# The second of two MLPs computed as seven half-size products, with combined weights kept in DRAM

## The chip, the cores and the metric

One core of a Trainium2 chip (trn2) runs the whole program. The metric is the device time of one execution in microseconds (us), from the core's first instruction to its last. The engines named below are TensorE (PE: matrix products; the loads of its weights are a row of their own, PEld), VectorE (DVE), ScalarE (ACT), GpSimd (POOL), and SyncE (SP), whose queue issues nearly all DMAs.

## The reference, cut to what matters

Block-causal attention (4 batches, 8 heads, 576 positions, head size 64; 64-wide blocks) gives x with 2304 tokens of width 512. Then two MLPs of inner width 2048 follow one another:

```python
attn = softmax(where(block_i >= block_j, q @ k.T / 8, -1e9)) @ v      # [4, 8, 576, 64]
x = attn.transpose(0, 2, 1, 3).reshape(2304, 512)
h = x @ moe_w_in;  r = maximum(h, 0)                 # [2304, 2048]
x = (s * (r * r) + b) @ moe_w_out                    # [2304, 512]
h = x @ moe2_w_in; g = maximum(0.01 * h, h)
out = g @ moe2_w_out
```

Inputs of the weights are 64-bit words that hold floating-point numbers; the kernel decodes them to 32 bits on the chip. Every product of the MLPs is carried in a high part and a low part: A B is computed as Ah Bh + Ah Bl + Al Bh, three matmuls for one.

## The kernel before, in words

Tokens are cut into five blocks by position in the sequence: four of 512 columns (4 batches of 128 positions) and one of 256 (NB = 5). The inner width is cut into 16 chunks of 128 (NF = 16). For one block and one chunk, `m_in` (L772) makes the hidden chunk h with 12 matmuls (four slices of 128 inputs, three matmuls each, L782), ACT and DVE apply the activation and split the result into high and low (`gh`, `gl`), and `m_out` (L817) adds it to four output banks y with 12 more (L831). So a chunk is 24 matmuls as wide as the block, and an MLP is 16 chunks of this for each of five blocks.

ORDER (L177) lists the ten blocks: five of the first MLP, in the order 0, 1, 2, 4, 3, then five of the second. While a block of the first MLP runs, the attention of the next block is worked off beside it, 16 pieces for each block (`later_block`, L584); so attention ends before the last block of the first MLP begins. The output of the first MLP is stored to DRAM (yT, L854) and read again by `x_split` (L738).

The weights lie in the pool "w", 16 buffers of 8 KB per partition, one for each chunk. `first_weights` (L323) and `second_weights` (L341) load 512 KB at a time and `chunk` (L268) decodes them: on DVE L275, L278, L286 and L294, on ACT L283 and L291, each over 1024 columns. The second MLP's chunks are loaded and decoded as the first MLP's last block gives up its buffers.

Nothing of this runs in the order in which it is written. `Graph.order` (L71) plays the steps through with an assumed length for each, gives each free engine the ready step with the earliest due time, and writes the steps out in that order; a step that opens a buffer waits until the pool has one free. The order on each engine is then fixed, and each engine works its own list from the top. The pool "st" has two buffers, through which y is evicted and stored.

## Time and profile before

| | |
|---|---|
| runs of the kernel | 993.75, 995.41 and 996.36 us, median 995.41 |
| span of the profiled execution | 995.1 us |
| busy share of the span | PE 99%, PEld 82%, DVE 48%, ACT 45%, POOL 10% |
| mean granted TensorE clock | 0.996 of full |
| DMA traffic | 83.91 MB, mean 84 GB/s |

The page gives the profiled execution by its span alone; the three runs lie around it. In the page's 40 slices of the span PE is at 9 tenths or more in all but the first and the last, and DVE falls from 4 to 9 tenths in the first 25 slices to 1 to 3 in the last 15, where only the second MLP runs.

### The profile page before, as it was taken

The page shows a single profiled execution, that of the slowest core. Times are in us where ns is not written, and L with a number is a line of the kernel's source. Part 1 is how long each engine was busy: PE and PEld are TensorE (multiplying, and loading weights), DVE is VectorE, ACT ScalarE, POOL GpSimd, SP SyncE. Part 2 cuts the span into 40 slices and gives each one's busy share as a digit, 9 for nine tenths or more (in the row PEclk, how much of TensorE's full clock was granted, in tenths as well). Part 3 has the DMA queues.
Part 4 walks back from the last instruction along what each step waited for, and adds up shares of the span by engine and source line. Part 5 has one row for each costly group of instructions (what it writes and reads, how often), then busy time and mean ns, then how long its engine had stood idle before and what let it go on. Part 6 is the DMA issues. An engine that isn't in the chain of part 4 may idle for free.

```text
span 995.1 us, 15325 instructions
## 1 busy us (share of the span) xinstructions
PE 980.2 (99%) x5684; PEld 815.2 (82%) x5684; DVE 478.9 (48%) x973; ACT 448.6 (45%) x975; POOL 99.0 (10%) x233
## 2 busy tenths in 40 slices
PE   9899999999999999999999999999999999999997
PEld 8688887777778888888878888888888888888897
DVE  5899865454566455756547996213112111311221
ACT  4777654454544455666636675213213121321221
POOL 1111411111121111222200000000000000000000
PEclk9999999999999999999999999999999999999999
DMA  8982232222233223433134563002001100200010
GB/s 198 329 282 78 62 112 83 64 57 66 73 107 99 72 83 88 121 105 105 57 107 171 209 222 117 1 1 84 1 1 54 32 1 1 64 1 1 12 32 22
DMA packets 84554, 83.91 MB, mean 84 GB/s; under 512 B 20352, under 2 KB 67584, under 8 KB 84480
## 3 DMA queue, kind: packets, MB, share of 16 engines
q1 hardware_dynamic: 82032, 82.15, 26.9%
q10 hardware_dynamic: 2448, 0.79, 0.3%
q8 instruction: 45, 0.74, 0.3%
q14 instruction: 29, 0.24, 0.1%
HBM read 73.47 MB, written 9.44 MB: 83 GB/s over the span
## 4 chain that ended last, share of the span: by engine, by line
PE 93%; DMA 4%; ACT 1%; SPq 1%; DVE 1%; issue 0%; POOLq 0%; ACTq 0%; DVEq 0%; POOL 0%
PE h L782 40%; PE y L831 39%; PE o L716 5%; PE t L454 4%; PE s L637 2%; DMA early<-in_moe_w_out_dram 2%; PE s L677 1%; PE s L439 1%; DMA fv<-in_v_dram 1%; DMA q<-in_q_dram 1%; DMA fk<-in_k_dram 1%; DVE g L798 0%; ACT g L800 0%; DMA out_dram<-yo 0%; SPq L309 0%
## 5 line engine op out<-in xcount | busy, mean ns | idle before, releaser
L782 PE MATMUL h<-xh,w 128*128 128x512 f32 (+1 forms) x1280 | 444.6, 379 | 3.5 <-ACT w L291 1.2
L831 PE MATMUL y<-gh,w 128*128 128x512 f32 (+2 forms) x1280 | 369.8, 372 | 0.0
L782 PEld LDWEIGHTS h<-xh,w 128*128 128x128 f32 x1280 | 237.7, 189 | 51.9 <-issue 5.3
L831 PEld LDWEIGHTS y<-gh,w 128*128 128x128 f32 x1280 | 230.0, 189 | 40.4 <-issue 1.0
L782 PE MATMUL h<-xl,w 128*128 128x512 f32 (+1 forms) x640 | 236.7, 370 | 0.5 <-DVE xl L552 0.5
L831 PE MATMUL y<-gl,w 128*128 128x512 f32 (+2 forms) x640 | 236.2, 369 | 0.2 <-DVE gl L811 0.2
L811 DVE TENSOR_TENSOR gl<-g,gh 128x512 fp32r<-128x512 f32 (+1 forms) x80 | 51.1, 639 | 275.8 <-ACT g L810 270.1
L809 ACT ACTIVATE gh<-h 128x512 fp32r<-128x512 f32 (+1 forms) x80 | 44.3, 554 | 273.1 <-PE h L782 273.1
L831 PEld LDWEIGHTS y<-gl,w 128*128 128x128 f32 x640 | 120.7, 189 | 20.9 <-DVE gl L811 0.4
L782 PEld LDWEIGHTS h<-xl,w 128*128 128x128 f32 x640 | 121.2, 189 | 17.9 <-DVE xl L552 0.9
L800 ACT ACTIVATE g<-h 128x512 f32<-128x512 f32 (+1 forms) x80 | 44.4, 555 | 109.2 <-PE h L782 102.4
L454 PE MATMUL t<-id_sb,p 128*128 128x128 f32 x400 | 65.2, 278 | 2.7 <-POOL p L656 2.0
L454 PEld LDWEIGHTS t<-id_sb,p 128*128 128x128 f32 x400 | 47.8, 141 | 18.4 <-ACT pt L370 3.3
L803 DVE TENSOR_TENSOR gl<-g,gh 128x512 fp32r<-128x512 f32 (+1 forms) x80 | 50.7, 634 | 12.8 <-ACT gh L802 12.4
L656 POOL TENSOR_SCALAR p<-p,l 128x384 f32<-128x384 f32 (+1 forms) x63 | 40.7, 659 | 159.2 <-DVE l L654 118.7
L798 DVE TENSOR_TENSOR g<-g,h 128x512 f32<-128x512 f32 (+1 forms) x50 | 30.3, 606 | 53.8 <-ACT g L800 53.6
L802 ACT ACTIVATE gh<-g 128x512 fp32r<-128x512 f32 (+1 forms) x80 | 47.0, 587 | 14.9 <-DVE g L798 14.2
L372 DVE COPY pt<-t 128x512 f32<-128x512 f32 (+2 forms) x54 | 31.8, 589 | 40.8 <-PE t L454 40.1
L716 PEld LDWEIGHTS o<-pt,v 128*64 128x64 f32 x896 | 41.4, 138 | 10.3 <-DVE pt L372 2.5
L716 PE MATMUL o<-pt,v 128*64 128x128 f32 (+1 forms) x896 | 48.3, 259 | 0.3 <-ACT pt L370 0.3
L810 ACT ACTIVATE g<-h 128x512 f32<-128x512 f32 (+1 forms) x80 | 44.0, 550 | 0.0
L370 ACT ACTIVATE pt<-t 128x512 f32<-128x512 f32 (+2 forms) x66 | 35.0, 532 | 19.9 <-PE t L454 18.2
(88 smaller groups left out, 884.2 us busy)
## 6 DMA issues: line engine op xcount, KB each, us to landing
early<-in_moe_w_in_dram SPq DMA_DIRECT2D x30, 512.0 KB, 3.8
early<-in_moe_w_out_dram SPq DMA_DIRECT2D x30, 512.0 KB, 4.6
v<-in_v_dram SPq DMA_DIRECT2D x32, 256.0 KB, 3.2
k<-in_k_dram SPq DMA_DIRECT2D x32, 144.0 KB, 2.9
yT<-yo SPq DMA_DIRECT2D x16, 256.0 KB, 2.4
k<-in_k_dram SPq DMA_DIRECT2D x32, 128.0 KB, 2.8
xf<-yT SPq DMA_DIRECT2D x16, 256.0 KB, 2.8
out_dram<-yo SPq DMA_DIRECT2D x16, 256.0 KB, 2.6
```

The source lines that it names most:

```text
L370: e.activation(out=out, in_=in_, func=ACTF.Copy, scale=by)
L454: e.transpose(tb()[:, x * 128:(x + 1) * 128], P()[:, pc:pc + 128], id_sb)
L656: G.add({"POOL": pool(nk), "DVE": dve(nk, 2)}, lambda e, h=h, l=l, P=P: e.tensor_scalar(out=P()[:, nk * h:nk * h + nk], in0=P()[:, nk * h: ...
L716: e.matmul(out=o()[64 * h:64 * h + 64, n * x:n * x + n], lhsT=V()[:, j, 64 * h:64 * h + 64], rhs=r, start=(j == 0), stop=(j == nj - 1),)
L782: e.matmul(out=h()[:, :T], lhsT=w()[:, wi, c * 128:(c + 1) * 128], rhs=x[blk, c]()[:, :T], start=(c == 0 and n == 0), stop=(c == KD - 1 an ...
L800: a = G.add({"ACT": act(T)}, lambda e: e.activation(out=g()[:, :T], in_=h()[:, :T], func=ACTF.Relu), [prev], [g], [h], due)
L802: hi = G.add({"ACT": act(T)}, lambda e: e.activation(out=gh()[:, :T], in_=g()[:, :T], func=ACTF.Copy), [a], [gh], [g], due)
L803: lo = G.add({"DVE": dve(T)}, lambda e: e.tensor_tensor(out=gl()[:, :T], in0=g()[:, :T], in1=gh()[:, :T].bitcast(F32), op=ALU.subtract), [ ...
L809: hi = G.add({"ACT": act(T)}, lambda e: e.activation(out=gh()[:, :T], in_=h()[:, :T], func=ACTF.Lrelu), [prev], [gh], [h], due)
L810: a = G.add({"ACT": act(T)}, lambda e: e.activation(out=g()[:, :T], in_=h()[:, :T], func=ACTF.Lrelu), [prev], [g], [h], due)
L811: lo = G.add({"DVE": dve(T)}, lambda e: e.tensor_tensor(out=gl()[:, :T], in0=g()[:, :T], in1=gh()[:, :T].bitcast(F32), op=ALU.subtract), [ ...
L831: e.matmul(out=y()[:, :W], lhsT=w()[:, wi, d * 128:(d + 1) * 128], rhs=x()[:, :W], start=(f == 0 and n == 0), stop=(f == NF - 1 and n == 2),)
```

## The change

The first MLP, the attention and their blocks stay as they are. The second MLP is computed another way, and the weights are handled another way.

**Seven products instead of eight.** The 2304 columns are taken as three groups j of 768, the inner width as two halves of 1024. A group and a half is one of six steps (STEPS). In a step, both matrix products are cut into 2 x 2 blocks, and Strassen's form (with Winograd's sums) makes the four result blocks from seven block products of 384 columns (NH = 384). One unit of PE work, called a product below, is six matmuls of 384 columns (L1088 for the input side, L1154 for the output side). The input side of a step is four groups `in_pair` of seven products; the output side, `out_phase`, is 28 products, seven for each of four groups. So a step is 56 products or 336 matmuls, and the second MLP is 2016 matmuls of 384 columns.

**Sums beside it.** The seven right-hand sides are made on the chip. `x_load` reads four quarters of the group's x for each of two slices and makes seven splits with four differences each: 22 instructions on ACT and 22 on DVE for each j, in 29 buffers "X" that serve one j at a time. For the output side each group needs four differences on DVE and seven splits (ACT the high part gh, DVE the low part gl, L1147 and L1001). Products that share a bank are chained: a bank is copied out by ACT before the next product is added onto it, and other banks are added to the result on DVE (L1063, L1068).

**Weights.** `units` loads the second MLP's weights in 16 units during the first MLP, decodes each, makes seven combinations (on DVE L424, L427, L433, four sums of 256 columns L441, one L448 over 1792 columns; on ACT two instructions), and stores them to DRAM (u_in, u_out, 29.4 MB). `load_units` reads them back in the second MLP, 15 loads of about 1 MB whenever the half changes, four times in all.

**Room.** The pool "w" has 12 buffers in place of 16. Eight of the first MLP's chunks are kept in DRAM too, and each later block reads four of them back (`weights_at`), walking the chunks back and forth. The SBUF of the attention's pools and of the first MLP's is given to the second MLP's pools; `gate` holds the opening of these until every step that uses the old ones has been issued. On the left side the old pools are stg, gh, gl, g, st, xh, xl and the new ones w2, gh2, gl2, Y, G; counted in KB per partition, st lies at 42 to 46 and the first of the 16 buffers of G at 43.5 to 45.

The diff, cut to its core:

```diff
+    def gate(self, fn, keys, new):
+
+        s = self.add({"X": 0.001}, fn, due=-1e9)
+        for u in self.steps:
+            if u is not s and any(b.key in keys for b in u.uses):
+                u.later.append(s)
+                s.left += 1
+        for k in new:
+            self.gates[k] = s
...
-                    dma = max(dma, end + 0.5) + s.nbytes / 220e3
+                    dma = max(dma, end + 0.5) + s.nbytes / 300e3
...
-ORDER = (0, 1, 2, 4, 3, 0, 1, 2, 3, 4)
+ORDER = (0, 1, 2, 4, 3)
...
-    EARLY = NF - 1
+    KEEP = 4
...
+    MLP1 = (("stg", 2), ("gh", 2), ("gl", 2), ("g", 1), ("st", 2), ("xh", 4), ("xl", 4))
+    ATT = (("xf", 4), ("k", 2), ("kh", 1), ("kl", 1), ("q", 3), ("qs", 1), ("v", 3), ("p", 2), ("pt", 3), ("sm", 6))
+    MLP2 = (("w2", 3), ("gh2", 3), ("gl2", 2), ("Y", 4), ("G", 16))
+    XIN = (("X", 29),)
+    open_pools("mlp1", "left", MLP1)
+    open_pools("att", "right", ATT)
...
-    def second_weights():
...
+            if f < KEEP or f >= NF - KEEP:
+                slot = f if f < KEEP else f - NF + 2 * KEEP
+                kept_ok[f] = G.add(
+                    {"SP": 0.65}, lambda e, w=w, slot=slot: e.dma_start(out=kept[slot], in_=w().bitcast(F32).rearrange("p a n -> p (a n)")),
+                    [a], [], [w], due + 8, nbytes=1048576)
...
+    def weights_at(blk, pos, f):
+
+        if not blk:
+            return
+        if pos < NF - KEEP:
+            w_t[blk, f] = w_t[blk - 1, f]
+            for i in range(2):
+                w_ok[blk, f, i] = w_ok[blk - 1, f, i]
+            return
+        slot = f if f < KEEP else f - NF + 2 * KEEP
+        w = w_t[blk, f] = buf("w", [128, 4, 512], F32R, "w")
+        a = G.add(
+            {"SP": 0.65}, lambda e: e.dma_start(out=w().bitcast(F32).rearrange("p a n -> p (a n)"), in_=kept[slot]),
+            [kept_ok[f], done[blk, pos - NF + KEEP]], [w], [], at(blk, pos) - 30, nbytes=1048576)
+        for i in range(2):
+            w_ok[blk, f, i] = a
...
+    def units():
+
+        seq = [(half, kind, i) for half in range(2) for kind in range(2) for i in range(4)]
...
+            slot = buf("stg", [128, 2, 2, 1024], F32, "unit")
...
+            s1 = comb("S1", "A21", "A22", ALU.add, [a])
+            s3 = comb("S3", "A11", "A21", ALU.subtract, [a])
+            s2 = comb("S2", "S1", "A11", ALU.subtract, [s1])
+            s4 = comb("S4", "A12", "S2", ALU.subtract, [s2])
+            hi = G.add({"ACT": act(1792)}, lambda e, c7=c7, h7=h7: e.activation(out=h7().bitcast(F32R), in_=c7(), func=ACTF.Copy), [s3, s4], uses=[slot], due=due)
+            lo = G.add({"DVE": dve(1792)}, lambda e, c7=c7, h7=h7: e.tensor_tensor(out=c7(), in0=c7(), in1=h7(), op=ALU.subtract), [hi], uses=[slot], due=due, port=True)
...
-    second_weights()
...
+    G.gate(lambda e: (close_pools("att"), open_pools("xin", "right", XIN)), [k for k, _ in ATT], [k for k, _ in XIN])
+    G.gate(lambda e: (close_pools("mlp1"), open_pools("mlp2", "left", MLP2)), [k for k, _ in MLP1], [k for k, _ in MLP2])
...
+    ONE = 6 * (NH / 2400 + 0.013)
+    IN_ORDER = (1, 5, 6, 3, 7, 2, 4)
+    STEPS = ((0, 0), (0, 1), (1, 1), (1, 0), (2, 0), (2, 1))
+    t2 = [begin[NB] + n * 56 * ONE for n in range(len(STEPS) + 1)]
...
+    def load_units(n):
+
+        j, half = STEPS[n]
+        if n and STEPS[n - 1][1] == half:
+            for m in (in_w, in_ok):
...
+                w = in_w[n, i, c] = buf("w", [128, 2, 7, 128], F32R, "wi")
+                in_ok[n, i, c] = G.add(
+                    {"SP": 0.65}, lambda e, w=w, u=8 * half + 2 * i + c: e.dma_start(
+                        out=w().bitcast(F32).rearrange("p s r n -> p s (r n)"), in_=u_in[u]),
+                    [*unit_ok[half, 0, i], *gate()], [w], [], t2[n] + 7 * ONE * i - 14, nbytes=917504, behind=line[-1:])
...
+                    raw[a, b] = buf("X", [128, NH], F32, "xr")
+                    row, col = (2 * (a - 1) + c) * 128, 2 * NH * j + NH * (b - 1)
+                    from_ = [y_st[k, 2 * (a - 1) + c] for k in range(NB) if T0[k] < col + NH and T0[k] + TB[k] > col]
+                    t += 0.01
+                    ld = G.add(
+                        {"SP": 0.65}, lambda e, x=raw[a, b], row=row, col=col: e.dma_start(out=x(), in_=yT[row:row + 128, col:col + NH]),
+                        [*from_, in_last[0]], [raw[a, b]], [], t - 4, nbytes=512 * NH)
...
+            a = split(1, x11, [ok[1, 1]])
+            t1 = comb(x11, x12, x11, [a, ok[1, 2]])
+            a = split(5, x11, [t1])
+            tt2 = comb(x11, x22, x11, [a, ok[2, 2]])
+            split(6, x11, [tt2])
+            a = split(2, x21, [ok[2, 1]])
+            t4 = comb(x21, x21, x11, [a, tt2])
+            t3 = comb(x12, x22, x12, [t1, ok[2, 2]])
+            split(7, x12, [t3])
+            split(4, x21, [t4])
+            split(3, x22, [ok[2, 2]])
...
+    def in_pair(n, i):
+
+        j = STEPS[n][0]
+        t = t2[n] + (7 * i + 2 * max(i - 1, 0)) * ONE
+        A, B, C = bank("h" if i % 2 == 0 else "t", "A"), bank("s", "B"), bank("s", "C")
+        where = {1: (A, True), 6: (A, False), 7: (A, False), 4: (A, False), 5: (C, True), 3: (C, False), 2: (B, True)}
...
+            def fn(e, r=r, x=x, first=first, ai=ai):
+                for c in range(2):
+                    hi, lo, _ = x2[j, r, c]
+                    for m, (s, y) in enumerate(((0, hi), (0, lo), (1, hi))):
+                        e.matmul(out=x()[:, :NH], lhsT=in_w[n, i, c]()[:, s, ai], rhs=y(), start=(first and c == 0 and m == 0), stop=(c == 1 and m == 2),
+                                 skip_group_check=True)
+
+            after = [*[in_ok[n, i, c] for c in range(2)], *[x2[j, r, c][2] for c in range(2)]]
+            after += {6: [ev.get(1)], 7: [ev.get(6)], 4: [ev.get(7)], 3: [ev.get(5)]}.get(r, [])
+            p = G.add({"PE": ONE}, fn, after, [x] * first, [x, *[in_w[n, i, c] for c in range(2)], *[q for c in range(2) for q in x2[j, r, c][:2]]], due)
...
+            if r in (1, 5, 6):
+                y = g[{1: (1, 1), 5: (2, 2), 6: (1, 2)}[r]]
+                ev[r] = G.add({"ACT": act(NH)}, lambda e, x=x, y=y: copy(e, y(), x()[:, :NH]), [p], [y], [x], d2)
+            elif r in (2, 3, 7):
+                y = g[{2: (1, 1), 3: (1, 2), 7: (2, 2)}[r]]
+                ev[r] = a = G.add({"DVE": dve(NH)}, lambda e, x=x, y=y: add(e, y(), x()[:, :NH]), [p, ev[{2: 1, 3: 6, 7: 5}[r]]], [], [x, y], d2)
+                ok[{2: (1, 1), 3: (1, 2), 7: (2, 2)}[r]] = G.add(
...
+    def out_phase(n):
...
+                gh, gl = buf("gh2", [128, NH], F32R), buf("gl2", [128, NH], F32R)
+                hi = G.add({"ACT": act(NH)}, lambda e, gh=gh, x=x: e.activation(out=gh(), in_=x(), func=ACTF.Copy), [a], [gh], [x], due - 2)
+                lo = G.add({"DVE": dve(NH)}, lambda e, gh=gh, gl=gl, x=x: sub(e, gl(), x(), gh().bitcast(F32)), [hi], [gl], [gh, x], due - 1.5, port=True)
...
+                def fn(e, r=r, i=i, z=z, first=first, gh=gh, gl=gl):
+                    for d in range(2):
+                        for m, (s, y) in enumerate(((0, gh), (1, gh), (0, gl))):
+                            e.matmul(out=z[d]()[:, :NH], lhsT=out_w[n, r]()[:, 2 * i + d, s], rhs=y(), start=(first and i == 0 and m == 0), stop=(i == 3 and m == 2),
+                                     skip_group_check=True)
...
+                if again and r in last:
+                    store(j, last[r], d, a, due + 2 * ONE)
```

What this does to the order on the engines shows at two places.

The first place is the border between the two MLPs, on ACT. Before, the last rows of the first MLP (y evicted into yo, L370) and the first of the second (L809, L810) follow one another with work for the weights between them:

```order
L802 ACTIVATE gh<-g 128x512 [waits Activation_49]
L283 ACTIVATE early<-early 128x1024 [waits DMAHW7_49,DMAHW6_49,DVE_49]
L370 ACTIVATE yo<-y,s_sb 128x512 [waits PE_49]
L291 ACTIVATE w<-early 128x2x512 [waits DVE_49]
L809 ACT_TABLE_LOAD
L809 ACTIVATE gh<-h 128x512 [waits PE_49]
L810 ACTIVATE g<-h 128x512 [waits Activation_49]
```

Now (the last split of the first MLP, one y, then the first copies of a bank A or C into G):

```order
L892 ACTIVATE gh<-g 128x512 [waits DVE_49]
L479 ACTIVATE yo<-y,s_sb 128x512 [waits DMAHW3_49,PE_49]
L1063 ACTIVATE G<-A 128x384 [waits DMAHW3_49,DMAHW2_49,DMAHW7_49,DMAHW0_49,DVE_49]
L1063 ACTIVATE G<-C 128x384
L1103 ACT_TABLE_LOAD
L1103 ACTIVATE G<-G 128x384 [waits DVE_49]
L1063 ACTIVATE G<-A 128x384 [waits PE_49]
L1147 ACTIVATE gh_7222<-G 128x384 [waits Activation_49]
```

The first copy into G now waits for four DMAs. SP's list at the same place shows which have these four numbers last (wo are weights of the output side, 1 MB each; before, no load stood between the stores of the border that anything on ACT waited for):

```order
L996 DMA wo<-u_out 128x2048 [waits DMAHW6_49,PE_49]
L936 DMA yT<-yo 128x512 [waits DMAHW7_49,DVE_49]
L936 DMA yT<-yo 128x512 [waits DMAHW0_49,Activation_49]
L996 DMA wo<-u_out 128x2048 [waits DMAHW1_49,PE_49]
L936 DMA yT<-yo 128x512 [waits DMAHW2_49,DVE_49]
L936 DMA yT<-yo 128x512 [waits DMAHW3_49,DVE_49]
```

A DMA's own number is the one that it waits for: the copy stands behind all four stores of the last block. On PE three products of the first group stand ahead of the last twelve matmuls of y, one product of the second group behind them, and then the product that needs this copy.

The second place is the change from one group j to the next, on DVE. Before, a change of block in the second MLP put four splits of x and four evictions among one gl for each chunk:

```order
L811 TENSOR_TENSOR gl<-g,gh 128x512 x14
L764 SCALAR_TENSOR_TENSOR xl<-xf,c_sb,xh 128x512 x4
L811 TENSOR_TENSOR gl<-g,gh 128x512
L372 COPY yo<-y 128x512 x2
```

Now, twelve rows of the stretch in which the second j's x is made (xr, xl) beside the output side of the first (gl, Y):

```order
L1001 TENSOR_TENSOR xl_8140<-xr,xh_8128 128x384
L1001 TENSOR_TENSOR gl_8143<-G,gh_8130 128x384
L1001 TENSOR_TENSOR xr<-xr 128x384
L1001 TENSOR_TENSOR G<-G 128x384
L1001 TENSOR_TENSOR xr<-xr 128x384
L1001 TENSOR_TENSOR xl_8160<-xr,xh_8156 128x384
L1001 TENSOR_TENSOR gl_8164<-G,gh_8158 128x384
L1001 TENSOR_TENSOR xr<-xr 128x384
L1001 TENSOR_TENSOR gl_8175<-G,gh_8162 128x384
L1001 TENSOR_TENSOR gl_8179<-G,gh_8166 128x384
L1001 TENSOR_TENSOR xl_8189<-xr,xh_8177 128x384
L1068 TENSOR_TENSOR Y<-A,Y 128x384
```

Four of these twelve are a gl that a product waits for; the rest stand in between. Counted in the lists, DVE has 68 instructions of 384 columns between one gl and the gl of the product 26 products later at each of the two changes of j; where j does not change, some 40 in such a stretch.

## Rows read from the trace of the kernel before

**Rows 1.** The page's chain of work that ended last, by engine.
```profile
PE 93%; DMA 4%; ACT 1%; SPq 1%; DVE 1%; issue 0%; POOLq 0%; ACTq 0%; DVEq 0%; POOL 0%
```
**Rows 2.** Windows: stretch, length, busy us (instructions) of each engine, clock, DMA.
```profile
50.00:100.00 50.00, 49.94 (x263) 40.68 (x258) 45.73 (x68) 38.27 (x65) 7.26 (x17) 1.00 0.53 178
100.00:500.00 400.00, 396.27 (x2785) 324.04 (x2783) 235.83 (x614) 219.69 (x546) 82.46 (x190) 1.00 0.30 84
595.00:989.00 394.00, 393.76 (x1916) 333.23 (x1915) 91.39 (x135) 103.27 (x192) 0.00 (x0) 1.00 0.09 27
```
**Rows 3.** Timeline of PE (start, us, instruction): 18 matmuls of 512, then 24 of 256.
```profile
587.80 0.39 PE L782 MATMUL h<-xh,w 128*128 128x512 f32 x1
...
591.88 0.39 PE L782 MATMUL h<-xh,w 128*128 128x512 f32 x1
...
965.72 0.28 PE L782 MATMUL h<-xh,w 128*128 128x256 f32 x1
...
968.60 0.28 PE L782 MATMUL h<-xh,w 128*128 128x256 f32 x1
```
**Rows 4.** Groups by line and shape: count, busy us, mean ns, idle before.
```profile
L570 DVE TENSOR_TENSOR kl<-k,kh 128x384 fp32r<-128x384 f32 x16 | 8.8, 551 | 0.2 <-ACT kh L569 0.2
L569 ACT ACTIVATE kh<-k 128x384 fp32r<-128x384 f32 x16 | 8.2, 511 | 0.0
```
**Rows 5.** Timeline of DVE: instructions that start behind one another.
```profile
427.64 0.41 DVE L798 TENSOR_TENSOR g<-g,h 128x256 f32<-128x256 f32 x1
427.97 0.28 DVE L567 SCALAR_TENSOR_TENSOR qs<-q,qs 128x128 fp32r<-128x128 f32 x1
...
570.20 0.69 DVE L275 TENSOR_SCALAR early<-early 128x1024 int32<-128x1024 int32 x1
570.92 1.23 DVE L278 SCALAR_TENSOR_TENSOR early<-early 128x1024 int32<-128x1024 int32 x1
572.07 0.68 DVE L803 TENSOR_TENSOR gl<-g,gh 128x512 fp32r<-128x512 f32 x1
572.67 1.22 DVE L294 TENSOR_TENSOR w<-early,w 128x1024 fp32r<-128x1024 f32 x1
573.81 1.22 DVE L286 SCALAR_TENSOR_TENSOR early<-early 128x1024 int32<-128x1024 int32 x1
```
**Rows 6.** Timeline of the end of the kernel.
```profile
988.80 0.28 PE L831 MATMUL y<-gl,w 128*128 128x256 f32 x1
990.87 0.42 DVE L372 COPY yo<-y 128x256 f32<-128x256 f32 x1 [2.40 <-DMA out_dram<-yo]
991.55 0.42 DVE L372 COPY yo<-y 128x256 f32<-128x256 f32 x1 [0.26 <-DMA out_dram<-yo]
```
**Rows 7.** The page's DMA issues: KB each, median us to landing.
```profile
early<-in_moe_w_in_dram SPq DMA_DIRECT2D x30, 512.0 KB, 3.8
...
yT<-yo SPq DMA_DIRECT2D x16, 256.0 KB, 2.4
...
out_dram<-yo SPq DMA_DIRECT2D x4, 128.0 KB, 2.3
```
**Rows 8.** Windows of 4 us around a late softmax, columns as in rows 2.
```profile
496.00:500.00 4.00, 2.66 (x21) 2.27 (x19) 1.36 (x4) 3.75 (x10) 1.25 (x2) 1.00 0.00 0
500.00:504.00 4.00, 3.30 (x14) 2.53 (x15) 2.23 (x5) 1.03 (x2) 0.81 (x3) 0.78 0.32 75
504.00:508.00 4.00, 4.00 (x44) 3.60 (x43) 0.94 (x3) 0.86 (x2) 0.00 (x0) 0.79 0.48 158
```
**Rows 9.** Timeline: the two waits of PE in that stretch.
```profile
499.50 0.33 PE L454 MATMUL t<-id_sb,p 128*128 128x128 f32 x1 [1.16 <-POOL p L656]
...
500.62 0.55 PE L454 MATMUL t<-id_sb,p 128*128 128x128 f32 x3 [0.79 <-POOL p L656]
```
**Rows 10.** Timeline: the last matmul of an h, and ACT's first read of it.
```profile
644.73 0.39 PE L782 MATMUL h<-xh,w 128*128 128x512 f32 x1
...
645.15 0.60 ACT L809 ACTIVATE gh<-h 128x512 fp32r<-128x512 f32 x1 [5.03 <-PE h L782]
```

More of the change, by code (lines that the diff above doesn't have):

```diff
@@ L248 @@
     begin, ut, t = [], [], 30.0
-    for k in range(2 * NB):
+    for k in range(NB):
         begin.append(t)
@@ new lines, in square @@
+        def square(e):
+            if e is nc.scalar:
+                e.activation(out=g()[:, :T], in_=g()[:, :T], func=ACTF.Square)
+            else:
+                e.tensor_tensor(out=g()[:, :T], in0=g()[:, :T], in1=h()[:, :T], op=ALU.mult)
+        a = G.add({"ACT": act(T)}, lambda e: e.activation(out=g()[:, :T], in_=h()[:, :T], func=ACTF.Relu), [prev], [g], [h], due)
+        a = G.add(both(T), square, [a], uses=[g, h], due=due)
+        hi = G.add({"ACT": act(T)}, lambda e: e.activation(out=gh()[:, :T], in_=g()[:, :T], func=ACTF.Copy), [a], [gh], [g], due)
@@ L839, in m_out @@
+                [y] * (pos == 0), [y, w, gh, gl], due + d * 0.01,
             )
             y_last[blk, d] = a
[L841 removed]
+            if pos < NF - 1:
                 continue
             o = buf("st", [128, 512], F32, "yo")
[L844 to L850 removed]
@@ L865 @@
-    second_weights()
-    for blk in range(2 * NB):
+            ev = G.add(both(T), lambda e, o=o, y=y: evac(e, o()[:, :T], y()[:, :T], s_sb), [a, *sb_ok], [o], [y], due)
+            if k == NB - 1:
+                c_ok.append(G.add({"DVE": 0.2}, lambda e, y=y, d=d: e.tensor_scalar(
+                    out=c_sb[:, d:d + 1], in0=y()[:, T:T + 1], scalar1=b_sb, scalar2=None, op0=ALU.mult), [a, *sb_ok], uses=[y], due=due))
+            rows = slice(d * 128, (d + 1) * 128)
+            y_st[k, d] = G.add(
+                {"SP": 0.65}, lambda e, o=o, rows=rows: e.dma_start(out=yT[rows, T0[k]:T0[k] + T], in_=o()[:, :T]),
+                [ev], uses=[o], due=due, nbytes=512 * T,
+            )
@@ L867 @@
+        done[blk, pos] = a
+    units()
+    for blk in range(NB):
         if blk:
@@ new lines, in store @@
+    def store(j, ab, d, a, due):
+        y = yt[j, ab]
+        rows = slice((2 * (ab[0] - 1) + d) * 128, (2 * (ab[0] - 1) + d + 1) * 128)
+        c0 = 2 * NH * j + NH * (ab[1] - 1)
+        for k in range(NB):
+            lo, hi = max(c0, T0[k]), min(c0 + NH, T0[k] + TB[k])
+            if lo >= hi:
+                continue
+            b0, b1 = (lo - T0[k]) // NQ[k], (hi - T0[k]) // NQ[k]
+            G.add(
+                {"SP": 0.65}, lambda e, k=k, lo=lo, hi=hi, b0=b0, b1=b1: e.dma_start(
+                    out=outT[rows].rearrange("m (b s) -> m b s", b=B)[:, b0:b1, 128 * k:128 * k + NQ[k]],
+                    in_=y()[:, d, lo - c0:hi - c0].rearrange("m (b s) -> m b s", s=NQ[k])),
+                [a], uses=[y], due=due, nbytes=512 * (hi - lo),
+            )
@@ L874 @@
+    for n in range(len(STEPS)):
+        if n == 0 or STEPS[n][0] != STEPS[n - 1][0]:
+            x_load(STEPS[n][0])
+        load_units(n)
+        for i in range(4):
+            in_pair(n, i)
+        out_phase(n)
     with tc.manual_schedule():
@@ L876 @@
             s.fn(E[s.on])
+    for group in list(opened):
+        close_pools(group)
 def kernel(q, k, v, moe_w_in, moe_w_out, moe_s, moe_b, moe2_w_in, moe2_w_out):
```

414 lines of the change are left out of this document (269 added, 145 removed).

## Prediction, made before the changed kernel ran

> **What bounds the kernel now.** First the chain of work that ended last: 93% of it is PE, and DMA, the next, has 4% [rows 1]. So I read where PE is not busy, and how long one of its matmuls takes. The windows show PE busy for 393.76 of the last 394.00 us, in which only the second MLP runs, and for 396.27 of the 400 us of attention and first MLP ahead of it, at the full clock [rows 2]. PE is the bound throughout, and a wait costs time only where PE stands. The pitch of its matmuls, start to start without a gap, is (591.88 − 587.80)/18 = 0.2267 us for 512 columns and (968.60 − 965.72)/24 = 0.120 for 256 [rows 3]; the 0.39 and 0.28 printed there are durations of matmuls that overlap. PE's last matmul starts at 988.80 [rows 6], so it is done at 988.92; the span ends 6.2 us later, at 995.1. All sums below are made against this span; the median of the runs, 995.41, lies 0.3 above it, and I add that at the end.
>
> **The matmuls of the second MLP.** Before: 1536 × 0.2267 + 384 × 0.120 = 394.3 us, which is the window of rows 2. So the rest, up to the border of the two MLPs, is 988.92 − 394.3 = 594.6 us. After: 2016 matmuls of 384 columns. No row has a matmul of that width; the line through the two pitches gives 0.1733, and 2016 × 0.1733 = 349.4 us. The bounds are the two pitches themselves. What could hold it above the line is the loading of weights, one load for each matmul: but at 256 columns such a load goes with a matmul every 0.120 us [rows 3], so it does not limit at 384. I take 349.4. **Gain: 44.9 us.** What follows is what eats of it.
>
> The Trainium skill (TensorE: Matmul & The Clock Gate, in Part 1, on the clock gate) has back-to-back matmuls at N/2.4 GHz plus 2.5 ns, an estimate of 0.1625 us for 384 columns, with which this term would be 328. The trace does not bear that out at its own widths: the formula makes 0.216 and 0.109 where rows 3 have 0.227 and 0.120.
>
> **The border of the two MLPs.** PE now needs, one product (6 × 0.1733 = 1.04 us) behind the last matmul of y, a copy into G that stands on ACT behind all four stores of the last block; ACT's other copies, SP's later loads and so the second group are queued behind it. The nearest rows are those of the kernel's end: four evictions through two st buffers, with stores in between (DVE waits 2.40 us for one [rows 6]), 6.2 us from the last matmul to the end. Those were 256 columns wide; at 512, two evictions take some 0.27 us longer each (0.68 [rows 5] against 0.42 [rows 6]) and two stores 0.1 each (2.4 against 2.3 [rows 7]): 6.9. The copy takes 0.51 [rows 4] and its release 0.1, and one product covers 1.04: PE idles 6.5 us. After such idling the clock falls: around the waits of 1.16 and 0.79 us [rows 9] it is 0.78 and 0.79 over two windows of 4 us [rows 8], which is half of full for a part of each and a loss of 4 × 0.22 + 4 × 0.21 = 1.7 us. That is 8.2. One of the wo loads of 1 MB stands between the stores in SP's list; from 256 KB in 2.4 us and 512 KB in 3.8 [rows 7], it would need some 6.6 and could hold the last two stores by 0 to 4.2 us. It has run for some 3 us when they are issued, so I take 0.6. **+8.8 us**, between 6 (no clock loss, quick stores) and 12.4.
>
> **The two changes of j.** DVE has 68 instructions of 384 columns between a gl and the gl 26 products on, and PE does these in 26 × 1.04 = 27.0 us. DVE's start-to-start is shorter than the printed duration: 0.33 for 256 columns, 0.60 for 512, 1.14 for 1024 [rows 5], so 0.465 for 384 on that line; the duration is 0.551 [rows 4]. 68 × 0.465 = 31.6 and 68 × 0.555 = 37.7. Some 1.4 us are covered by two gl buffers filled ahead. That leaves 31.6 − 27.0 − 1.4 = 3.2, up to 9.3, for each change; I take 6.5, the middle, because instructions that wait for ACT do not go at the shortest pitch. **+13 us** for both (6.4 to 18.6; clock losses as above would add up to 3.4). Elsewhere 40 instructions in such a stretch take 40 × 0.465 = 18.6 to 22.2 us, below 27, and cost nothing.
>
> The Trainium skill (VectorE: DVE Perf Modes, The DRAIN you can't avoid) says that the next operation does not start until the pipe is empty. By that the duration is the pitch, and this term is 18.6 in place of 13. The trace disagrees on the kernel's own instructions: 0.60 us from start to start behind one that is recorded with 0.68 [rows 5].
>
> **Small waits.** In each of 24 groups `in_pair`, four products wait for an ACT or DVE result of an earlier one, with one product between. From the start of an earlier product's last matmul to the dependent product is 0.17 + 1.04 = 1.21 us. ACT starts 0.42 after the start of that matmul [rows 10], its copy takes 0.51 [rows 4], the release 0.1: 0.2 us of slack. Where a split of gh (another 0.51) stands ahead on ACT, 0.3 is lost. 24 × 4 waits at 0 to 0.15 each are 0 to 14 us. **+6 us**, nearer to nothing since half of ACT's time is free.
>
> **The first MLP.** The 16 units of weights put onto DVE, each: 0.72 + 2 × 1.14 + 4 × 0.33 + 1.95 (the 1792 columns, on the line of rows 5) = 6.3 us, 100 us in all, beside 235.83 that stand in the 400 us from 100 on [rows 2]: 84% busy. In the 50 us before, DVE is at 45.73 of 50 already [rows 2], and eight stores of kept chunks join the loads there in SP's list, which works from the top. So the softmax, whose steps DVE shares, can be late more often than before. One such event costs 1.16 + 0.79 [rows 9] + 1.7 of clock [rows 8] = 3.65 us. I take two, **+7 us**, between −1 (decoding of the second weights leaves the last block) and +20. What hides the remaining unit work, its DMAs included (four loads, two or four stores per unit on SP), is that DMA runs at 0.30 of its engines in this stretch [rows 2]. The reloads of kept chunks and the 60 reloads in the second MLP, where DMA is at 0.09, are due some 14 to 30 us ahead; I count them as nothing; if that cover went, a load of 1 MB is the 6.6 us above.
>
> **The end.** The last results are two adds on DVE, each with its store, and no st buffer is waited for. A first read follows the last matmul's end by some 0.3 us (0.42 from its start [rows 10]), the adds take 0.465 + 0.551, and from the end of the last eviction, 991.55 + 0.42 [rows 6], to the end of the span there are 3.1 us: 4.4 in place of 6.2.
>
> **Sum.** 594.6 + 7 + 8.8 + 349.4 + 13 + 6 + 4.4 = 983.2 us; with the 0.3, **983.5**.
>
> **Rivals.**
> *Little is eaten.* The waits lie at their low ends: border 6, changes of j 6.4, small waits 0, first MLP 0: 594.6 + 6 + 349.4 + 6.4 + 4.4 = 961. For it: DVE's short pitch is measured; PE was covered before with 99% busy. Against it: the border wait is in the order, and nothing covers it. Chance 0.2.
> *The full DVE duration is the pitch* (the rule above): 983.5 + 5.6 = 989.1. Against it: rows 5. Chance 0.05, and it stays faster.
> *Slower: late softmax in the first MLP.* Place: blocks 1 to 3, where 48 attention pieces run beside the units. DVE works its list in order, so a piece whose exponential sum waits behind one unit instruction of 1.14 or 1.95 us is late by that, and PE, with nothing else in its list, stands. Price 3.65 us each. Without the first-MLP term the sum is 976.5; six events bring 998.4, so it decides from six of 48 pieces; eight give 1005.7. For it: 91% of DVE in 50 to 100 us and 84% after. Against it: the units' steps have far due times, and before, PE lost only 3.73 of 400 us at 59% of DVE [rows 2]. Chance 0.2.
> *Seven products do not save* because a matmul of 384 columns goes at the pitch of 512: 2016 × 0.2267 = 457, and 1091 in all. Only if the pitch did not follow the width, which 0.120 at half the width excludes [rows 3]. Chance below 0.01.
>
> **How the numbers follow.** The forecast with terms around their middles, 970 to 992, has 0.45, the DRAIN case 0.05; the low rival 0.2; between 992.4 and 998.4, three to five late pieces, 0.1; slower 0.2. What a measurement of this kernel can tell from no change is about 0.3%, 3 us: faster is 0.45 + 0.05 + 0.2 = 0.70, same 0.10, slower 0.20. For 8 in 10 the range goes to both rivals: 960 to 1006, as both hold 0.2 and half of each lies inside or at the ends.
>
> **What would show it.** After: the pitch of PE within a product 0.173 us; a gap of some 6 us on PE behind the last y, released by ACT's copy into G and that by the DMA of yT, with a clock near 0.8 after it; two stretches with DVE above 95% and PE waiting for gl, 6 us each; no gap elsewhere above 0.5; PE busy in 100 to 500 us for 390 or more. Wrong would be: many PE waits for softmax rows between 100 and 500; PE waiting for DMA of wi or wo; a pitch above 0.18.

## The result, and the profile after

| | before | after |
|---|---|---|
| median of the runs | 995.84 us (993.75 to 996.36, 4 runs) | 980.0 us (977.85 to 982.65, 4 runs) |
| ratio of after to before | | 0.9843, 95% interval 0.9821 to 0.9865 |
| span of the profiled execution | 995.1 us | 975.9 us |
| PE / DVE / ACT busy | 99 / 48 / 45% | 97 / 67 / 59% |
| DMA traffic | 83.91 MB | 197.26 MB |

The changed kernel takes 1.6% less time, and the interval is clear of 1. The row of before has one run more than the section ahead of the prediction. Medians and ranges in this document are those of the fast runs; one of the six runs of the last experiment, c1_all, took 2217.23 us and is left out. Each run's time is 1.8 to 2.0 us more than its span, and the profiled execution (977.85 us) is the fastest of the four, so the profile below shows the change at its best: 19 us of span, where the medians differ by 16.

Windows of the profile after; columns as in rows 2. The stretch from 602 on is the second MLP.

```profile
50.00:100.00 50.00, 49.92 (x279) 40.37 (x279) 44.04 (x75) 39.81 (x74) 12.01 (x24) 1.00 0.69 233
100.00:500.00 400.00, 390.79 (x2689) 315.72 (x2689) 305.84 (x671) 272.26 (x596) 82.97 (x175) 1.00 0.78 240
602.00:972.00 370.00, 355.42 (x2012) 349.44 (x2010) 228.10 (x442) 196.52 (x406) 0.00 (x0) 0.99 0.43 157
```

Against rows 2, PE stands 9.2 us in 100 to 500 us (before 3.7) and 14.6 us in the second MLP (before 0.2). DVE has 306 us of work in the 400, in place of 236, and DMA is at 0.78 of its engines in place of 0.30. PE's only wait directly for a DMA is 0.6 us for q at the start. The longest of its waits in the changed kernel, by what ended them (us in total, times, longest):

```profile
PE A L1088 <- ACT G L1063: 6.6, 1, 6.6
PE C L1154 <- DVE gl L1001: 4.2, 5, 1.6
PE h L874 <- DVE g L888: 3.5, 3, 1.9
PE B L1154 <- DVE gl L1001: 1.9, 2, 1.0
PE t L563 <- POOL p L765: 1.9, 4, 0.9
PE h L874 <- ACT g L890: 1.6, 2, 1.3
PE A L1154 <- ACT gh L1147: 1.5, 2, 0.8
```

Three places stand out, and each is one that the prediction has a term for: the border (G), the changes of j (gl and gh), and the activations and the softmax in the first MLP (g, p).

**The border.** Timeline of all engines there (start, us, engine, line, instruction, idle time before and its releaser):

```profile
604.59 0.39 PE L917 MATMUL y<-gl,w 128*128 128x512 f32 x1
...
605.90 1.51 DVE L483 TENSOR_SCALAR yo<-y,s_sb 128x512 f32<-128x512 f32 x2 [2.17 <-DMA yT<-yo]
606.67 1.08 SPq L936 DMA_DIRECT2D yT<-yo  x2
...
612.11 0.49 ACT L1063 ACTIVATE G<-A 128x384 f32<-128x384 f32 x1 [7.77 <-DMA yT<-yo]
...
612.66 0.69 PE L1088 MATMUL A<-xh,wi 128*128 128x384 f32 x1 [6.62 <-ACT G L1063]
```

The last matmul of y is done at 604.82. The last two evictions wait for a store to free their buffer, the last two stores are issued behind them, and only when these have landed does ACT make its first copy into G; PE waits for that copy. The matmul at 612.66 is recorded with 0.69 us where others have 0.34. Windows around it, the last one of the stretch at the lower clock alone (the clock is the third number from the right, DMA's share the second):

```profile
608.00:612.00 4.00, 0.00 (x0) 0.00 (x0) 0.00 (x0) 0.00 (x0) 0.00 (x0) 0.61 0.98 373
612.00:616.00 4.00, 3.34 (x11) 3.35 (x12) 0.56 (x1) 3.58 (x6) 0.00 (x0) 0.54 1.01 424
616.00:620.00 4.00, 4.00 (x25) 4.00 (x24) 2.88 (x6) 1.95 (x5) 0.00 (x0) 1.00 0.60 235
608.86:615.68 6.82, 3.02 (x9) 3.02 (x10) 0.56 (x1) 3.38 (x6) 0.00 (x0) 0.50 0.99 401
```

PE's clock is at its lower level, 0.50 of full, from 608.86 us, in the gap, to 615.68; most matmuls behind the gap are 0.32 us apart until then, and that costs another 1.5 us. The DMA engines are full meanwhile, with loads of wo: SP issues four, of 1 MB each, between 605.0 and 610.1 us.

**The pitch.** PE in the last products:

```profile
967.88 0.51 PE L1154 MATMUL A<-gh,wo 128*128 128x384 f32 x2
...
971.52 0.51 PE L1154 MATMUL A<-gh,wo 128*128 128x384 f32 x2
971.87 0.34 PE L1154 MATMUL A<-gl,wo 128*128 128x384 f32 x1
```

From the start at 967.88 to the one at 971.52 there are 21 matmuls: 3.64/21 = 0.1733 us, to the last digit the line through the two pitches of rows 3. PE is done at 972.04, 3.9 us ahead of the end.

**The first change of j.** DVE works from 705 to 731 us with hardly a pause (the two longest are 0.29 and 0.17 us); a part of that:

```profile
707.32 1.01 DVE L1068 TENSOR_TENSOR Y<-C,Y 128x384 f32<-128x384 f32 x2
708.25 0.55 DVE L1001 TENSOR_TENSOR xl<-xr,xh 128x384 fp32r<-128x384 f32 x1
708.72 0.55 DVE L1001 TENSOR_TENSOR gl<-G,gh 128x384 fp32r<-128x384 f32 x1
709.18 0.55 DVE L1001 TENSOR_TENSOR xr<-xr 128x384 f32<-128x384 f32 x1
```

The start-to-start is 0.47 us for a duration of 0.55, as the line through rows 5 had it (0.465). By the starts of PE's matmuls beyond 0.1733 each, PE loses 5.7 us at each of the two changes. The last step, which no change of j follows, loses 0.9 at the same place: that much belongs to the second half of each group, where DVE adds to Y what ACT copies in the first.

**The rest.** In the other stretches of the second MLP the starts show hardly any loss, some 0.3 us in all.

### The profile page after: what moved, and what is told of

Its sections match the earlier page's. It is cut to its first block, busy times and chain, and to the rows that moved or that the text cites. A ratio compares the mean times of both kernels' runs of the same rounds, so it can differ in the third digit from the quotient of the medians.

```text
span 975.9 us, 16708 instructions
## 1 busy us (share of the span) xinstructions
PE 942.3 (97%) x5780; PEld 828.6 (85%) x5780; DVE 657.4 (67%) x1343; ACT 576.3 (59%) x1247; POOL 106.2 (11%) x231
## 2 busy tenths in 40 slices
DMA packets 143828, 197.26 MB, mean 202 GB/s; under 512 B 23296, under 2 KB 118144, under 8 KB 137088
## 5 line engine op out<-in xcount | busy, mean ns | idle before, releaser
L874 PE MATMUL h<-xh,w 128*128 128x512 f32 (+1 forms) x640 | 231.1, 390 | 5.1 <-DVE g L888 3.5
L917 PE MATMUL y<-gh,w 128*128 128x512 f32 (+1 forms) x640 | 186.0, 374 | 0.2 <-ACT gh L892 0.2
L874 PEld LDWEIGHTS h<-xh,w 128*128 128x128 f32 x640 | 118.4, 189 | 31.3 <-issue 5.2
L917 PEld LDWEIGHTS y<-gh,w 128*128 128x128 f32 x640 | 114.5, 188 | 22.2 <-issue 2.3
L1147 ACT ACTIVATE gh<-G 128x384 fp32r<-128x384 f32 x168 | 86.8, 524 | 59.1 <-PE A L1154 25.5
L1001 DVE TENSOR_TENSOR gl<-G,gh 128x384 fp32r<-128x384 f32 x168 | 92.5, 554 | 43.3 <-PE A L1154 18.7
L1088 PE MATMUL A<-xh,wi 128*128 128x384 f32 x384 | 112.9, 337 | 6.6 <-ACT G L1063 6.6
L874 PE MATMUL h<-xl,w 128*128 128x512 f32 (+1 forms) x320 | 118.5, 370 | 0.6 <-DVE xl L857 0.6
L917 PE MATMUL y<-gl,w 128*128 128x512 f32 (+1 forms) x320 | 118.5, 370 | 0.3 <-DVE l L763 0.3
L1154 PE MATMUL A<-gh,wo 128*128 128x384 f32 x384 | 98.4, 337 | 1.5 <-ACT gh L1147 1.5
L1088 PEld LDWEIGHTS A<-xh,wi 128*128 128x128 f32 x384 | 71.1, 189 | 7.0 <-ACT G L1063 6.9
L1154 PEld LDWEIGHTS A<-gh,wo 128*128 128x128 f32 x384 | 69.0, 188 | 2.8 <-ACT gh L1147 2.1
L1154 PE MATMUL A<-gl,wo 128*128 128x384 f32 x192 | 64.7, 337 | 0.4
L1088 PE MATMUL A<-xl,wi 128*128 128x384 f32 x192 | 64.7, 337 | 0.0
```

Of the source, the lines that this page charges most:

```text
L874: e.matmul(out=h()[:, :T], lhsT=w()[:, wi, c * 128:(c + 1) * 128], rhs=x[blk, c]()[:, :T], start=(c == 0 and n == 0), stop=(c == KD - 1 an ...
L917: e.matmul(out=y()[:, :W], lhsT=w()[:, wi, d * 128:(d + 1) * 128], rhs=x()[:, :W], start=(pos == 0 and n == 0), stop=(pos == NF - 1 and n ...
L1001: e.tensor_tensor(out=out, in0=x, in1=y, op=ALU.subtract)
L1088: e.matmul(out=x()[:, :NH], lhsT=in_w[n, i, c]()[:, s, ai], rhs=y(), start=(first and c == 0 and m == 0), stop=(c == 1 and m == 2), skip_g ...
L1147: hi = G.add({"ACT": act(NH)}, lambda e, gh=gh, x=x: e.activation(out=gh(), in_=x(), func=ACTF.Copy), [a], [gh], [x], due - 2)
L1154: e.matmul(out=z[d]()[:, :NH], lhsT=out_w[n, r]()[:, 2 * i + d, s], rhs=y(), start=(first and i == 0 and m == 0), stop=(i == 3 and m == 2) ...
```

## Experiments

In all of them the time is that of one execution where one run is named, and a loss is taken from the starts of PE's matmuls, as above. "The first MLP's end" is the end of its last matmul of y less the 3.1 us of the three products that stand ahead of it: 604.82 − 3.12 = 601.7 in the changed kernel, against 594.6 in the sum's first step.

**b1_pools: G no longer shares bytes with st.**

```diff
-    MLP2 = (("w2", 3), ("gh2", 3), ("gl2", 2), ("Y", 4), ("G", 16))
+    MLP2 = (("G", 16), ("w2", 3), ("gh2", 3), ("gl2", 2), ("Y", 4))
```

> Only the place of the second MLP's pools in SBUF changes: G stands first and no longer shares bytes with st, so the first copy into G waits for no store; the order on every engine is the same as in the changed kernel. My theory (the border is the wait of that copy for the four yT stores): the gap of 6.62 us on PE goes to under 0.5 us, the clock stays at 1.00 behind it (the half-clock stretch of 1.4 us goes too), and the time falls by 7 to 8.5 us. Rival (the border is bound by the loads of weights, whose DMA engines are 98% busy in 608 to 612 us, and the copy is only the first thing to show it): PE then waits for wi or wo a few products on, and the time falls by less than 3 us.

Measured: 971.86 us (970.75 to 972.65, 4 runs), 0.9751 of the runs of before taken with it (median 996.58), interval 0.9734 to 0.9769. PE and the clock at the border:

```profile
610.59 0.44 PE L1088 MATMUL A<-xh,wi 128*128 128x384 f32 x1 [0.70 <-ACT G L1063]
```

```profile
610.00:614.00 4.00, 3.41 (x20) 3.42 (x21) 2.50 (x5) 2.46 (x6) 0.00 (x0) 1.00 1.01 373
```

The gap is 0.70 us in place of 6.62, the clock stays at 1.00, and the loss of the 30 us behind the last y falls from 8.3 to 1.0 us. DMA is as full as before (1.01 of its engines), and PE doesn't wait for it. So the border is that one copy into bytes of st, and nothing else; one line is worth 8 us.

**b2_wo_behind: the stores ahead of the loads, G left where it was.**

```diff
-                [*[s for i in range(4) for s in unit_ok[half, 1, i]], *gate()], [w], [], t2[n] + 28 * ONE + 4 * ONE * o - 14, nbytes=1048576, behind=line[-1:])
+                [*[s for i in range(4) for s in unit_ok[half, 1, i]], *gate()], [w], [], t2[n] + 28 * ONE + 4 * ONE * o - 14, nbytes=1048576, behind=[*line[-1:], *([y_st[ORDER[-1], d] for d in range(KD)] if n == 0 else [])])
```

> G shares bytes with st as in the changed kernel, but the wo loads of 1 MB are issued behind the four yT stores of the last block instead of between them. In the changed kernel the last two stores took some 4.4 us to land (issued at 607.75 at the latest, the copy began at 612.11) where a store of 256 KB takes 2.4 at the median. If the loads in front of the stores make them late, the gap on PE falls from 6.6 to 4 to 5 us. Rival: the stores are bound by their two buffers and their own landing; the gap stays at 6 to 6.6 us. A wait of PE for wo may come in its place some 10 us later; if so I expect under 1 us of it.

Measured: 980.4 us (one run). The border:

```profile
613.21 0.49 ACT L1063 ACTIVATE G<-A 128x384 f32<-128x384 f32 x1 [5.19 <-DMA yT<-yo]
...
613.75 0.69 PE L1088 MATMUL A<-xh,wi 128*128 128x384 f32 x1 [4.04 <-ACT G L1063]
```

The gap is 4.0 us in place of 6.6: the loads of wo among the stores had cost 2.6. PE waits for no load of wo in their place. But more of the stretch with the low clock falls on matmuls here:

```profile
612.00:616.00 4.00, 2.25 (x7) 2.25 (x8) 0.56 (x1) 2.68 (x4) 0.00 (x0) 0.52 0.98 341
616.00:620.00 4.00, 4.00 (x17) 4.00 (x16) 1.46 (x3) 1.43 (x3) 0.00 (x0) 0.63 1.01 426
612.15:618.98 6.83, 5.23 (x16) 5.23 (x17) 1.47 (x3) 3.90 (x7) 0.00 (x0) 0.50 0.99 374
```

so that gap and clock together lose 6.7 us in place of 8.3. The time of this one run does not show that gain: its first MLP ended at 605.4 us, 3.7 later than in the changed kernel's profile.

**b3_x_early: x work may begin four products earlier.**

```diff
-            in_last[0] = p
+            if r == XGATE:
+                in_last[0] = p
...
+    XGATE = 6
```

> The loads of the next group's x wait for the third product of the last in_pair group instead of the seventh, so DVE may begin four products (4.2 us) earlier with the 22 instructions and ACT with its own 22. My theory (at a change of j DVE has more instructions than PE's products give it time for: it runs without a pause from 705 to 731 us at 0.468 us each): the loss of 5.7 us at each change falls to between 1.5 and 3 us, some 6 us in all. Rival (the loss comes from the order, x work standing in front of gl, whatever the time at hand): the loss stays at 5 to 6 us for each change.

Measured: 982.74 us (one run). It is worse: 7.4 and 7.0 us lost at the changes of j. PE's waits in the second MLP (the first is the border):

```profile
PE A L1089 <- ACT G L1064: 6.6, 1, 6.6
PE A L1156 <- DVE Y L1069: 3.0, 4, 1.1
PE C L1156 <- DVE gl L1001: 2.4, 3, 1.0
PE A L1156 <- ACT gh L1149: 1.5, 2, 0.7
PE A L1156 <- DVE gl L1001: 1.0, 2, 0.5
```

With more time for the same work, the x work only comes sooner and pushes evictions of Y behind it that PE did not wait for before. The loss also lies above the 5 to 6 us of the rival. What is added is the clock, which falls behind these waits at the first change and likewise, from 836.73 to 840.15 us, at the second; in the changed kernel it stays at 1.00 in both places:

```profile
713.85:717.27 3.42, 3.42 (x12) 3.42 (x11) 3.31 (x8) 1.91 (x6) 0.00 (x0) 0.50 0.00 0
```

By the starts of the matmuls the low clock costs some 1.4 us each time, and what is left, 5.9 and 5.6 us, is the loss of the changed kernel. So the theory that DVE lacks time fell here, and the rival stood: what stands in front counts.

**b4_x_late and b5_x_due_only: the same work, later.** Both on top of b1_pools. b5 changes the due times of x:

```diff
         for c in range(2):
+            t = t2[n0] - (10 if j else 24) + (0.8 * c if j else 0.6 * 7 * c)
...
-                t += 0.6
+                t += 1.6 if j else 0.6
```

and b4 besides lets the planner reckon with the start-to-start times, at these two lines and at every other ACT and DVE step of the second MLP alike:

```diff
-                a = G.add({"ACT": act(NH)}, lambda e: e.activation(out=hi(), in_=x(), func=ACTF.Copy), after, [hi], [x], t)
-                a = G.add({"DVE": dve(NH)}, lambda e: sub(e, lo(), x(), hi().bitcast(F32)), [a], [lo], [hi, x], t, port=True)
+                a = G.add({"ACT": (0.105 + NH / 1200)}, lambda e: e.activation(out=hi(), in_=x(), func=ACTF.Copy), after, [hi], [x], t)
+                a = G.add({"DVE": (0.068 + NH / 960)}, lambda e: sub(e, lo(), x(), hi().bitcast(F32)), [a], [lo], [hi, x], t, port=True)
```

> On top of b1_pools, with the same instructions in the second MLP: the planner reckons there with the start-to-start times that the trace shows (0.468 us on DVE and 0.425 on ACT for 384 columns, instead of 0.555 and 0.52), and the second and third group's x work is due later (from 10 us ahead of its step on, both slices side by side, instead of 24 us ahead, one slice after the other), so that a gl which a product waits for goes first. Theory after b3_x_early (the loss at a change of j is one of order: DVE has time enough, but x work stands ahead of gl): the two losses of 5.3 us fall to under 1.5 us each, the time falls by 8 to 10 us against b1_pools. Rival (DVE has too much to do between the two in_pair phases): the losses only move from gl to xl, PE waits at the start of the next in_pair for 3 us or more each, and the time falls by less than 4 us.

> As b4_x_late, but the planner keeps its longer assumed times; only the due times of the x work are changed. If the due times alone do it, the losses at the changes of j are as in b4_x_late, under 1.5 us each. If the planner, which believes DVE to be full where it is not, still puts the gl late, I expect 2 to 3.5 us each, half of the loss in b1_pools.

Measured: 967.42 us for b4 and 970.7 for b5 (one run each). PE's waits in the second MLP, b4:

```profile
PE A L1089 <- ACT G L1064: 1.3, 1, 1.3
PE C L1155 <- DVE gl L1001: 1.1, 3, 0.4
PE A L1089 <- ACT xh L1039: 0.6, 2, 0.3
```

and b5:

```profile
PE A L1089 <- DVE G L1069: 1.5, 2, 0.7
PE A L1155 <- DVE gl L1001: 1.1, 2, 0.6
PE C L1155 <- DVE gl L1001: 1.1, 3, 0.4
PE A L1089 <- ACT G L1064: 0.7, 1, 0.7
```

The losses at the two changes are 1.4 us each in b4 and 3.2 each in b5, against 5.7 each in b1. The number of instructions is the same in all, so DVE does have the time: the work of a change of j fits if a gl that is waited for goes ahead of an xl that is not. Of the 4.3 us that b4 gains at each change, 2.5 are the due times and 1.8 the assumed lengths (0.555 us for DVE, and ACT's with it), by which the planner held DVE for full. b4's time fell by 4.4 us, less than the 8 to 10 expected; its second MLP is 7.4 us shorter than b1's (the border costs 0.8 more), but its first ended at 606.0 us, 2.6 later than b1's with the same order of work (more on that spread below).

**u1_half_units: half of the units left out.** The second half of the second MLP uses the first half's weights again, so 8 of the 16 units aren't made.

```diff
-        seq = [(half, kind, i) for half in range(2) for kind in range(2) for i in range(4)]
+        seq = [(half, kind, i) for half in range(1) for kind in range(2) for i in range(4)]
-            due = t0 + (n + 1) * (t1 - t0) / len(seq)
+            due = t0 + (n + 1) * (t1 - t0) / 16
```

> Only the eight units of the first half of the inner width are made and stored; the second half of the second MLP reads the first half's weights again, so its output is another one. The units then end near 330 us instead of 495, and DVE is relieved by 8 x 6.3 = 50 us, ACT and the DMA likewise, in the 256-wide block (403 to 507 us) above all. My theory (the 7.1 us that the first MLP lost come from DVE and ACT work of the units standing ahead of the activation and the softmax there): PE's waits in 400 to 500 us fall from 7.8 to about 3 us as before, and the first MLP ends 4 to 6 us earlier. Rival (the reloads of kept weights and the 12 buffers cost it): waits in 400 to 500 us stay at 7 us or more.

Measured: 969.87 us (one run). The windows 400 to 500 us of before, the changed kernel and this one, each in its fence:

```profile
400.00:500.00 100.00, 97.11 (x876) 83.17 (x874) 63.20 (x178) 63.89 (x160) 26.16 (x62) 1.00 0.33 95
```

```profile
400.00:500.00 100.00, 92.19 (x803) 76.39 (x803) 78.06 (x186) 71.52 (x165) 26.37 (x57) 0.98 0.81 240
```

```profile
400.00:500.00 100.00, 98.03 (x881) 84.05 (x879) 63.92 (x181) 63.40 (x160) 25.93 (x62) 1.00 0.47 138
```

PE is back at 98.03 us, DVE and ACT are where they were before, and the first MLP ends at 593.9: earlier than before. The reloads of kept weights and the 12 buffers are all still there, so they cost nothing that PE sees. And the eight units that remain, between 150 and 330 us, cost nothing either. What is lost is lost beside the 256-wide block, where a chunk has half the PE time but the units' instructions are as long as ever: from the last matmul of y of the block ahead to its own, that block takes 99.9 us in the kernel before, 108.3 in the changed one and 98.7 here, and each of the other three blocks behind the first is within 0.6 us of before in both. How it comes about there, DVE in the changed kernel ahead of PE's longest such wait (1.90 us, ended by the last row):

```profile
453.43 1.21 DVE L433 SCALAR_TENSOR_TENSOR unit<-unit 128x1024 int32<-128x1024 int32 x1
...
455.35 0.69 DVE L481 COPY pt<-t 128x512 f32<-128x512 f32 x1 [0.71 <-PE t L563]
...
456.12 0.42 DVE L441 TENSOR_TENSOR unit<-unit 128x256 f32<-128x256 f32 x1
...
456.53 0.41 DVE L893 TENSOR_TENSOR gl<-g,gh 128x256 fp32r<-128x256 f32 x1
457.45 0.42 DVE L888 TENSOR_TENSOR g<-g,h 128x256 f32<-128x256 f32 x1 [0.51 <-ACT g L890]
```

and the ACT step that this g waits for:

```profile
457.03 0.38 ACT L890 ACTIVATE g<-h 128x256 f32<-128x256 f32 x1 [0.16 <-DVE gl L893]
```

Unit rows, attention rows and the activation of h stand in one list; the g of one chunk is begun only when the gl of the one before is through, and that stood behind unit and attention rows.

**u2_units_apart: all units, but not beside that block.** On top of b1_pools.

```diff
-            due = t0 + (n + 1) * (t1 - t0) / len(seq)
+            rel = 0.0
+            if n < 12:
+                due = t0 + (n + 1) * (begin[3] - 14 - t0) / 12
+            else:
+                rel = begin[4] - 8 + (n - 12) * 19
+                due = rel + 16
```

> On top of b1_pools: the 16 units are kept whole, but twelve are due by the end of the third block and the loads of the last four are held back to the start of the fifth block, so that hardly a unit runs beside the 256-wide fourth block (about 403 to 507 us). Theory (units beside that block are what the first MLP loses, as u1_half_units showed by leaving half of them out): PE's idle time in 400 to 500 us falls from 6.7 to 2 to 3 us, the clock there is 1.00 again, and the time falls by 4 to 7 us against b1_pools. Rival (it is the amount of unit work, wherever it lies): waits of the same size appear before 400 us or behind 507, and the time is within 2 us of b1_pools.

Measured: 967.58 us (one run).

```profile
400.00:500.00 100.00, 96.84 (x845) 82.11 (x845) 64.95 (x178) 63.12 (x162) 27.11 (x60) 1.00 0.53 157
```

PE's idle time there is 3.2 us in place of 6.7, the clock is 1.00, and the first MLP ends at 598.9, 4.5 us ahead of b1's. The 256-wide block takes 102.7 us, b1's 107.5; the blocks behind the first take 439.8 us together, against 446.3 in b1 and 438.8 before. So the place counts, not the amount.

**c1_all: the three together.**

> b1_pools, b4_x_late and u2_units_apart together. If the three losses are separate places, their gains add up: 971.9 less 8 to 10 less 4 to 7, some 956 to 960 us. If one only hides another, the sum falls short by the smaller of the two.

Measured: 960.1 us (958.06 to 962.99, 5 runs), 0.965 of the runs of before taken with it (median 995.53), interval 0.9637 to 0.9663, at the upper end of what was expected. The second MLP in the windows of its profile:

```profile
596.00:952.00 356.00, 353.12 (x2013) 349.22 (x2011) 227.39 (x442) 197.19 (x406) 0.00 (x0) 1.00 0.45 163
```

PE is idle for 2.9 us of it, where the changed kernel had 14.6. By the medians the time is 11.8 us below b1_pools, and the gains that u2 and b4 showed at their own places, 4.5 and 7.4, add up to 11.9. That they meet so closely is chance: 4.5 compares two single profiles, and before's own median differs by 1 us between the two sets of runs. In the profiles of b1_pools and c1_all themselves the blocks behind the first give 7.4 us and the second MLP 6.8. The three losses are separate places.

## Why the prediction was right, point by point

983.5 us was predicted, from 960 to 1006, and 980.0 measured; the change was 15.8 us by the medians, where the sum gave 11.9. The path was right: PE is the bound, the matmuls give what was worked out, and three of the places named eat of it. But the sum was better than some of its terms, and that is luck.

- **The matmuls:** right to the digit. 0.1733 us, so 349.4 us; the weight loads do not limit. Every matmul takes 13 ns beyond its columns at the full clock (2.4 GHz), at 256, 384 and 512 columns alike (0.120, 0.1733 and 0.2267 us). The Trainium skill's formula (TensorE: Matmul & The Clock Gate, Part 1) made it 0.1625, which the trace after does not bear out either.
- **The border:** +8.8 predicted, 8.3 measured (6.8 gap, 1.5 clock), by the mechanism named. Inside, two steps were off and cancelled: the stores by themselves make a gap of 4.0 us (b2), where I had 6.5 from the kernel's end, whose last 3.1 us hold more than a store's landing; and the wo loads cost 2.6 where I took 0.6 of a bound of 4.2. The release that I put at 0.1 without a row is 0.06 here (612.60 to 612.66). The clock of the windows around it is 0.61 and 0.54, not the 0.8 that was to show it, as the gap takes part of the low stretch.
- **The changes of j:** +13 predicted, 11.3 measured (and 0.9 more in the last step, which the sum did not have), but the step "68 instructions against 27.0 us" is right only as arithmetic. 68 × 0.468 = 31.8 us is 4.8 over, near the 5.7 that are lost; yet b4 does the same 68 with a loss of 1.4, because they need not be done within those 27 us. What I counted as a lack of time was an order. The reason for taking the middle, that instructions which wait for ACT do not go at the shortest pitch, does not hold either: they go at 0.47 us from start to start, for a recorded 0.55. The rival that the recorded duration is the pitch, 18.6 for this term, is out by the same rows. The prediction gave only half of the section that it cited there: the Trainium skill (VectorE: DVE Perf Modes, The DRAIN you can't avoid) goes on that a next operation that nothing holds back starts earlier. So these rows speak against the rival, not against the section.
- **The small waits:** +6 predicted, 0 measured. The slack is there (0.35 us, of which the sum put 0.1 to the release), but the step that failed is "a split of gh stands ahead on ACT": from 622 us on ACT either stands idle ahead of these copies (0.55 us in the row below) or has one other copy or activation of the same group there; a split of gh holds none of them up. The first matmul of product 6 starts at 628.74, 0.35 us after the copy that it needs is over:

```profile
627.52 0.34 PE L1088 MATMUL A<-xh,wi 128*128 128x384 f32 x1
...
627.90 0.49 ACT L1063 ACTIVATE G<-A 128x384 f32<-128x384 f32 x1 [0.55 <-PE A L1088]
...
628.74 0.34 PE L1088 MATMUL A<-xh,wi 128*128 128x384 f32 x1
```

- **The first MLP:** +7 predicted, 7.1 in the profiled execution, some 10 in a usual one: over the six profiles of kernels that differ from it only in the second MLP (the changed kernel, b1 to b5) the first MLP ends between 601.7 and 606.5 us, 604.4 on average. The 256-wide block alone takes 7.5 to 9.5 us more than before in these six. The size came out, but by a price for two late softmax pieces; in the trace 3.7 of PE's 8.8 us of waits in 400 to 510 us are for the activation of h (before: 0.4 of 3.1), the others mostly for the softmax. The other blocks behind the first lose nothing, but for 2 us in one of them in b4 and b5. DVE came to 76% of the 400 us, not 84. The slower rival had the right cause (unit work ahead of short steps on DVE) and looked at the wrong quantity, the share of DVE over 400 us, where the block with the shortest chunks decides.
- **The end:** 4.4 predicted, 3.9 measured.
- **From span to time:** 0.3 predicted; this step is wrong. Each run's time is about 1.95 us above its span (a run of before with a span of 995.1 took 996.98), so a span can't be set against a median of times as I did; and the profiled execution lies 2.1 below the median. Here the missing 3.8 us made up for half of the 7.3 by which the sum had the span too long (983.2 against 975.9). The number is nearer than its parts deserve.
- **The signs:** the pitch, the gap of some 6 us, the two stretches with DVE full, the loss of some 6 us at each and PE's 390 us in 100 to 500 (390.8) came as said. "No gap elsewhere above 0.5" did not: beside the 256-wide block there are waits of up to 1.9 us.

DMA went from 0.30 to 0.78 of its engines beside the first MLP, which I had not reckoned up, and still PE waited for none of it; in u1, at 0.47 of the DMA engines in 400 to 500 us, the reloads of kept weights alone cost PE nothing.

What stays open: why the first MLP's end moves by 4.8 us over those six profiles, with the same order of work but for its last steps in b4. Most of it is there early: the last matmul of y of the first block starts between 157.9 and 161.9 us, and from there to the last one of all it is 446.3 to 450.1 us. No run shows what moves the first block. Executions of one kernel differ as well: the runs of before lie 2.6 us apart (993.75 to 996.36), those of the changed kernel 4.8.

## What to carry to other kernels

When a change frees the engine that bounds the kernel, look for what it has left in the way at the borders: here three places gave back 20 of 45 us, none of them for lack of an engine's time. A buffer that shares bytes with one whose store is still under way, long side work put beside the block with the shortest steps, and side work due ahead of what is waited for were each worth 4 to 8 us by the time of a run, and each was mended in a line or a few. And a planner's assumed length should be the time from start to start, not the recorded duration.
